# A new written-out order for a two-layer long-convolution and MLP kernel, with eight warm-up matmuls for six

## The chip, the cores and the metric

The kernel runs on one core of one Trainium2 chip. The metric is the device time of one execution in microseconds (us). Times are compared as medians of several runs; one further execution of each kernel is recorded by the hardware profiler, and every duration below comes from such a record. The engines are TensorE (PE; its weight loads are listed as PEld), VectorE (DVE), ScalarE (ACT), GpSimd (POOL) and SyncE (SP), which here issues nearly all transfers between memory (HBM) and the on-chip buffer. Matmul results land in PSUM, eight banks of 512 float32 columns on 128 partitions, and must be copied out by ACT or DVE.

## The reference

Inputs are bfloat16: a sequence of 2048 positions with 512 channels, filters, and a two-matrix MLP with 1376 hidden units. The result is four residual steps, a convolution mixer and an MLP, twice:

```python
def _A_ref(q, k, v, shift_k, ssm_k, ssm_D):
    for t in range(4):                                   # a short filter over k, by channel
        k_shift = k_shift + k_pad[:, t:t+S, :] * shift_k[:, 3-t][None, None, :]
    kv = k_shift * v
    y = irfft(rfft(pad(kv)) * rfft(pad(ssm_k)))[:S]      # a convolution 2048 long, by channel
    y = y + kv * ssm_D
    return q * y
def _B_ref(x, w1, b1, w2, b2):
    h = gelu(layernorm(x) @ w1 + b1)
    return h @ w2 + b2
x = A_q
for _ in range(2):
    x = x + _A_ref(layernorm(x), A_k, A_v, A_shift_k, A_ssm_k, A_ssm_D)
    x = x + _B_ref(layernorm(x), B_w1, B_b1, B_w2, B_b2)
```

The convolution's output doesn't depend on x, so it is computed once and used by both layers.

## The kernel before, in words

**The front** computes the convolution by matmuls with constant matrices. Each stage is made of tiles: one PE operation of several matmuls into one or two PSUM banks, and one copy of it by ACT or DVE (`evac`, line 453).

- *Filter* (tag `ht`): the filter arrives in four blocks (SP transfers 5 to 8, 512 KB each), is transposed on PE in four operations of 16 (62, 65, 68, 71, line 528), copied, and gets D added in one row (70, 73 and on POOL 64, 67).
- *First transform of the filter* (`h1`, line 545): 16 operations (74 to 104, even numbers) of 16 matmuls with 64 columns of weights, copied by the operation one number on.
- *Second transform* (`h2`, line 558): 16 operations (106 to 136) of 8 matmuls with the tables of transfers 28 to 43; then 16 transfers on chip (138 to 153) make a copy with the halves exchanged.
- *Short filter of k, times v* (`fir0` to `fir3`): channels 0 to 255 on PE (two transposes 154 and 168, line 589, with their copies 155 and 169; four filter operations 156, 158, 170, 172, line 606, each followed by a product with v on DVE, 157, 159, 171, 173, line 613); channels 256 to 511 on DVE (182 to 189 and 198 to 205, line 450, 16 passes of 2048 columns). They need the loads of k (10 to 19) and v (20 to 27).
- *First transform of kv* (`x1`, line 545), *second transform and product with the filter's* (`x2`, line 651, with a product on DVE each; the last is 268 or 274), *two inverse stages* (`i1`, line 674; `i2`, line 731).

**The two layers** run in blocks of 1 or 2 (first layer) and 4 (second layer) row tiles of 128 positions: statistics (line 754, 756) and norm (768) on DVE, a power on POOL (760, 762), the product with y and the addition to x on DVE (line 450), statistics and norm again, a transpose (tiles 0 and 1 on PE, line 814; all others by SP transfers, line 807), the first MLP matrix in 11 operations of 4 matmuls (`m1`, line 827) with a gelu each on ACT (line 832), the second one in three operations of 4, 4 and 3 matmuls per row tile (`m2`, line 860) and the addition to x on DVE (line 864). The last row tile's m2 is cut into 256, 128 and 128 columns (lines 849 and 853) with a transfer of the result after each.

**What sets the order.** Nothing is scheduled by the chip or by a library. Each operation gets a number in the order in which the program's text makes it. Then `arrange` goes through the tuple `ORDER`, 1114 numbers, and appends each operation to its engine's queue; each engine works its queue off strictly in order. An operation that two engines could do has a first and a second choice, and `SECOND` lists those that take the second. `BANKS` gives each PSUM tile its first bank; an operation that opens a tile waits for the copies out of the bank's former tile. `sync` derives the semaphore waits from the data dependences. So `ORDER`, `SECOND` and `BANKS` decide the sequence on every engine, SP's transfers included, and nothing else does.

**The warm-up**: POOL clears a row of zeros (operation 47, line 493) and one of ones (`one`, operation 49, line 504, a memset of 1 x 128); PE multiplies the zeros (operation 48, line 499) ahead of the filter's transposes, which are made to follow it.

Of the kernel before, what the change touches and what calls it, by code (L numbers as in the profile page):

```python
# [38 lines left out]
class Prog:  # L39
# [3 lines left out]

    G = 4
    ORDER = (
        0, 47, 8, 7, 48, 5, 3, 71, 68, 72, 73, 6, 1, 62, 98, 104, 16, 2, 69, 4, 65, 15, 63, 70, 64, 53, 102, 11, 13, 32, 49, 57, 99, 66,
        105, 100, 101, 80, 103, 50, 81, 17, 67, 76, 74, 56, 9, 51, 90, 52, 77, 94, 91, 96, 75, 19, 14, 12, 36, 95, 44, 18, 25, 27, 78, 60,
        61, 43, 10, 79, 35, 45, 26, 24, 88, 59, 86, 97, 82, 89, 42, 87, 92, 83, 41, 40, 33, 21, 84, 93, 182, 55, 168, 169, 85, 54, 154, 198,
        29, 155, 114, 30, 199, 120, 121, 31, 183, 58, 172, 136, 115, 173, 130, 116, 184, 137, 132, 28, 117, 158, 133, 108, 131, 200, 109,
        134, 106, 185, 22, 34, 135, 122, 23, 159, 123, 201, 186, 118, 20, 39, 156, 119, 107, 112, 202, 110, 157, 38, 37, 113, 111, 140, 126,  # L50
        46, 166, 203, 162, 187, 167, 170, 164, 127, 204, 124, 171, 163, 141, 165, 294, 128, 174, 139, 180, 129, 125, 176, 175, 181, 188,
        160, 178, 138, 177, 205, 189, 208, 161, 210, 209, 179, 145, 211, 196, 217, 212, 146, 220, 197, 310, 148, 218, 213, 190, 219, 221,
        144, 149, 143, 214, 215, 192, 142, 222, 147, 306, 194, 223, 193, 206, 224, 191, 195, 225, 229, 216, 235, 230, 231, 298, 207, 236,
        232, 233, 226, 296, 153, 260, 263, 304, 237, 227, 305, 257, 234, 275, 299, 228, 264, 261, 269, 254, 151, 258, 265, 244, 150, 255,
        333, 259, 276, 242, 240, 262, 300, 245, 243, 152, 256, 272, 266, 270, 248, 267, 277, 271, 273, 274, 307, 241, 246, 297, 268, 252,
        250, 247, 238, 251, 376, 253, 334, 377, 335, 292, 249, 302, 419, 477, 288, 336, 308, 378, 337, 421, 239, 420, 290, 422, 278, 379,
        293, 313, 289, 291, 314, 282, 286, 280, 529, 279, 479, 423, 380, 531, 284, 283, 424, 287, 281, 315, 381, 319, 285, 323, 430, 325,
        382, 425, 316, 338, 339, 295, 385, 317, 342, 324, 331, 340, 320, 383, 326, 301, 329, 341, 384, 303, 343, 478, 318, 344, 426, 386,
        332, 530, 431, 345, 330, 427, 346, 387, 347, 433, 480, 327, 348, 532, 349, 388, 432, 428, 389, 390, 533, 328, 429, 438, 435, 434,
        436, 321, 309, 481, 370, 534, 368, 391, 354, 439, 371, 369, 482, 437, 350, 440, 535, 356, 483, 366, 355, 441, 351, 442, 352, 358,  # L60
        357, 392, 360, 484, 364, 353, 367, 372, 445, 312, 393, 359, 443, 395, 399, 322, 409, 394, 397, 538, 583, 485, 486, 396, 407, 446,
        400, 365, 536, 633, 581, 362, 408, 398, 539, 489, 487, 488, 537, 635, 361, 490, 491, 444, 363, 403, 634, 401, 410, 405, 415, 404,
        413, 311, 636, 406, 373, 540, 492, 411, 582, 493, 451, 449, 461, 452, 450, 374, 453, 543, 541, 412, 402, 455, 494, 467, 584, 495,
        585, 462, 497, 459, 586, 542, 587, 414, 544, 468, 463, 465, 590, 447, 687, 454, 637, 460, 448, 545, 457, 588, 496, 591, 546, 416,
        549, 638, 592, 456, 473, 685, 417, 458, 498, 469, 642, 547, 464, 470, 466, 639, 686, 688, 519, 513, 589, 514, 595, 550, 375, 640,
        593, 474, 505, 548, 517, 511, 506, 737, 594, 499, 471, 518, 501, 738, 789, 418, 500, 596, 555, 512, 520, 643, 597, 641, 645, 502,
        646, 561, 475, 689, 598, 559, 472, 551, 644, 647, 560, 503, 690, 791, 569, 509, 557, 793, 599, 504, 691, 507, 552, 739, 515, 648,
        694, 510, 508, 476, 649, 570, 600, 571, 553, 692, 794, 516, 521, 522, 601, 693, 525, 790, 650, 651, 556, 565, 554, 740, 563, 602,
        567, 795, 741, 566, 572, 558, 697, 796, 526, 792, 742, 653, 573, 562, 797, 698, 609, 798, 652, 623, 615, 564, 527, 574, 568, 523,
        743, 616, 575, 528, 617, 607, 695, 618, 746, 696, 699, 605, 621, 744, 576, 577, 603, 700, 745, 608, 604, 622, 871, 578, 747, 701,  # L70
        613, 606, 611, 612, 624, 702, 748, 654, 749, 655, 619, 873, 524, 656, 669, 610, 799, 659, 620, 703, 579, 665, 629, 675, 751, 750,
        802, 869, 752, 614, 753, 754, 657, 704, 630, 666, 580, 663, 673, 660, 664, 667, 705, 631, 757, 875, 755, 674, 805, 706, 808, 658,
        661, 668, 800, 874, 632, 809, 801, 662, 870, 625, 872, 671, 670, 756, 876, 626, 877, 709, 758, 676, 806, 672, 707, 627, 681, 677,
        708, 803, 810, 759, 725, 771, 807, 628, 878, 678, 682, 760, 815, 761, 710, 683, 772, 816, 879, 719, 811, 949, 726, 880, 817, 679,
        720, 812, 804, 723, 951, 762, 763, 813, 724, 882, 684, 711, 950, 680, 715, 717, 955, 885, 775, 886, 881, 764, 712, 888, 814, 818,
        953, 727, 721, 954, 779, 887, 769, 895, 765, 780, 713, 819, 891, 889, 722, 766, 952, 896, 883, 714, 767, 716, 781, 728, 729, 820,
        890, 823, 827, 770, 824, 768, 897, 777, 718, 773, 956, 884, 892, 776, 774, 957, 778, 893, 825, 958, 962, 959, 828, 894, 826, 730,
        785, 733, 963, 898, 968, 782, 965, 821, 786, 787, 822, 899, 783, 969, 734, 843, 960, 900, 901, 841, 784, 731, 849, 907, 847, 735,
        961, 966, 732, 964, 903, 831, 833, 788, 1029, 905, 736, 1030, 837, 850, 967, 908, 848, 829, 844, 835, 904, 971, 906, 975, 1031,
        1033, 976, 902, 1035, 836, 839, 970, 977, 911, 909, 1034, 838, 973, 913, 972, 840, 1036, 919, 834, 1032, 842, 830, 1037, 925, 1038,  # L80
        926, 920, 912, 1045, 978, 923, 914, 845, 1048, 915, 927, 921, 1042, 832, 974, 979, 846, 910, 1039, 917, 1046, 980, 983, 855, 864,
        984, 1040, 922, 918, 928, 1041, 1043, 851, 924, 929, 1047, 1049, 985, 865, 856, 1050, 1044, 987, 916, 1057, 1051, 857, 1052, 866,
        860, 858, 981, 940, 982, 1053, 988, 1054, 1055, 986, 931, 1056, 930, 932, 1058, 861, 1059, 1060, 933, 935, 944, 934, 989, 995, 941,
        1061, 942, 1062, 867, 990, 1009, 1065, 945, 852, 853, 1003, 936, 1004, 937, 996, 1001, 1063, 1002, 943, 991, 862, 1005, 1064, 1067,
        854, 938, 997, 1066, 1010, 999, 993, 1068, 1069, 863, 1081, 939, 992, 946, 947, 1085, 1000, 1077, 1071, 948, 994, 1006, 1070, 1087,
        1079, 1088, 1083, 998, 1073, 1078, 1007, 1020, 1074, 1075, 1082, 1008, 1089, 1024, 1080, 1072, 1086, 1076, 1015, 1016, 1090, 1084,
        1108, 1100, 1111, 1017, 1021, 1112, 1011, 1109, 1095, 1025, 1096, 1018, 1026, 1012, 1097, 1101, 1013, 1113, 1022, 1027, 1102, 1014,
        859, 868, 1098, 1019, 1091, 1023, 1110, 1103, 1028, 1104, 1092, 1093, 1094, 1105, 1099, 1106, 1107)
    SECOND = (
        63, 64, 66, 67, 69, 70, 72, 77, 85, 89, 91, 97, 101, 161, 179, 191, 197, 213, 251, 283, 324, 392)  # L90
    BANKS = (
        0, 2, 0, 2, 2, 0, 4, 0, 4, 6, 0, 2, 2, 6, 6, 4, 2, 0, 4, 4, 0, 6, 4, 6, 0, 6, 2, 6, 0, 4, 6, 4, 4, 6, 4, 2, 2, 0, 0, 2, 0, 4, 6, 2,
        2, 6, 0, 6, 0, 6, 0, 2, 6, 2, 4, 6, 2, 2, 4, 2, 0, 0, 4, 0, 0, 0, 4, 6, 2, 0, 2, 4, 2, 6, 0, 4, 2, 4, 2, 6, 2, 6, 4, 0, 2, 4, 0, 2,
        6, 0, 6, 4, 4, 0, 0, 4, 4, 2, 6, 0, 6, 2, 2, 0, 6, 3, 1, 3, 0, 5, 1, 2, 6, 2, 6, 7, 7, 3, 7, 2, 1, 2, 3, 3, 4, 3, 4, 7, 2, 5, 2, 5,
        1, 0, 0, 0, 4, 3, 3, 0, 1, 4, 2, 5, 4, 5, 6, 5, 4, 2, 2, 3, 7, 2, 2, 5, 4, 0, 7, 3, 5, 1, 4, 7, 6, 0, 0, 5, 4, 1, 3, 2, 5, 1, 2, 1,
        2, 6, 6, 3, 4, 5, 6, 0, 1, 1, 6, 2, 0, 0, 4, 3, 4, 0, 2, 0, 2, 5, 3, 1, 1, 5, 5, 0, 5, 6, 0, 0, 1, 7, 1, 6, 1, 3, 4, 6, 2, 7, 3, 0,
        5, 2, 4, 6, 7, 1, 4, 2, 0, 7, 3, 4, 7, 5, 4, 3, 6, 7, 2, 7, 6, 1, 0, 3, 1, 2, 1, 4, 6, 2, 0, 3, 0, 1, 2, 5, 5, 5, 2, 2, 1, 0, 4, 7,
        4, 6, 1, 1, 2, 5, 7, 3, 0, 4, 2, 1, 3, 2, 2, 3, 1)


    def __init__(self, nc):
# [393 lines left out]
    tl = Tile(2)  # L495

    def f(e, tl=tl, z=z):
        for i in range(6):
            r = e.matmul(Q(tl, 0, 128, 0, [1, 512]), z[:, :128], z, start=True, stop=True)
        return r  # L500
    warm = P.op(PE, f, reads=[z], tile=tl)
# [399 lines left out]
```

## Time and profile before

| | before |
|---|---|
| median of 3 runs (lowest to highest) | 243.98 us (243.57 to 245.47) |
| the profiled execution's own time | 242.91 us |
| its span, first to last instruction | 241.1 us |
| PE busy (2330 matmuls) | 228.3 us, 95% |
| DVE busy | 172.7 us, 72% |
| ACT busy | 140.0 us, 58% |
| granted TensorE clock | 1.00 |

The span leaves out 1.8 us around the instructions. Rows of the timeline and of the chain of waits begin with the start and the length of a piece in us; "x16" counts the instructions merged into it; brackets give the idle time before it and what ended it ("issue": nothing that the profile shows). A row of the waits reads: engine and line that waited, what it waited for, us in total, times, the longest. PE busy is a modelled figure, since matmuls overlap: what counts is the distance between the starts. The trace also has each transfer's landing and the transfers that bring PE's instructions (queue q8: 18 packets, 0.29 MB).

### The profile page before, as it was taken

What the parts mean: (1) busy time and instruction counts of PE and PEld (TensorE: products, weight loads), DVE (VectorE), ACT (ScalarE), POOL (GpSimd) and SP (SyncE); (2) the same over time, 40 slices, a digit from 0 to 9 for tenths busy, and PEclk for the clock granted to TensorE, in tenths of its full rate; (3) what the DMA queues carried; (4) which work ended last, traced back from release to release, by engine and by line L of the source; (5) the groups of instructions that cost most, each with busy time, mean ns of one, the idle gap of its engine ahead of it and who ended that gap; (6) DMA issues with size and microseconds to landing.
All of it is one profiled execution on the core that took longest, in us unless ns stands there. A gap on an engine that the chain in (4) does not pass through costs nothing.

```text
span 241.1 us, 5575 instructions
## 1 busy us (share of the span) xinstructions
PE 228.3 (95%) x2330; PEld 152.5 (63%) x2330; DVE 172.7 (72%) x358; ACT 140.0 (58%) x225; POOL 37.6 (16%) x78
## 2 busy tenths in 40 slices
PE   6996999887899999999999999999999999999995
PEld 3985777675799887577667658644444444444543
DVE  0799699999999999999699789968772532100133
ACT  2397999999999995446426524703584013638000
POOL 1283000000004260603411201220120100000000
DMA  6999924999992001220301110223110332010204
GB/s 239 352 380 365 386 77 121 294 229 290 336 382 65 3 7 39 45 46 13 76 0 26 34 31 3 44 45 65 24 22 0 65 68 65 0 43 0 101 0 163
DMA packets 37035, 27.40 MB, mean 114 GB/s; under 512 B 19506, under 2 KB 29969, under 8 KB 37010
## 3 DMA queue, kind: packets, MB, share of 16 engines
q1 hardware_dynamic: 36446, 26.91, 37.3%
q8 instruction: 18, 0.29, 0.5%
q10 hardware_dynamic: 564, 0.14, 0.4%
q14 instruction: 7, 0.06, 0.1%
HBM read 16.82 MB, written 2.10 MB: 78 GB/s over the span
## 4 chain that ended last, share of the span: by engine, by line
PE 79%; DVE 8%; ACT 8%; DMA 2%; issue 2%; DVEq 0%
PE ps L827 32%; PE ps L860 31%; ACT ar L453 8%; DVE ar L450 5%; PE ps L674 5%; PE ps L731 3%; PE ps L528 2%; PE ps L545 2%; DVE ar L613 2%; DMA ar<-in_A_ssm_k_dram 2%; PE ps L651 2%; PE ps L849 1%; DVE ar L453 1%; PE ps L589 1%; PE ps L606 1%
## 5 line engine op out<-in xcount | busy, mean ns | idle before, releaser
L832 ACT ACTIVATE ar<-ps,sm 128x256 bf16<-128x256 f32 (+5 forms) x143 | 64.2, 523 | 71.3 <-PE ps L827 58.1
L827 PE MATMUL ps<-ar 128*128 128x256 bf16 (+5 forms) x572 | 82.6, 297 | 0.1
L860 PE MATMUL ps<-ar 128*128 128x512 bf16 (+1 forms) x341 | 79.9, 379 | 0.0
L453 ACT ACTIVATE ar<-ps 128x1024 bf16<-128x1024 f32 (+3 forms) x81 | 74.7, 1059 | 8.4 <-PE ps L545 6.5
L827 PEld LDWEIGHTS ps<-ar 128*128 128x128 bf16 (+1 forms) x572 | 53.0, 100 | 29.5 <-ACT ar L832 0.8
L450 DVE TENSOR_TENSOR ar<-ar 128x512 bf16<-128x512 bf16 (+3 forms) x105 | 63.5, 637 | 0.5 <-ACT ar L453 0.2
L860 PEld LDWEIGHTS ps<-ar 128*128 128x128 bf16 (+1 forms) x341 | 33.0, 98 | 34.5 <-ACT ar L832 0.2
L864 DVE TENSOR_TENSOR ar<-ar,ps 128x512 bf16<-128x512 bf16 x31 | 20.9, 683 | 34.9 <-PE ps L860 34.8
L754 DVE BATCH_NORM_STATS2 sm<-ar 128x6 f32<-128x512 bf16 (+1 forms) x68 | 42.5, 649 | 0.2
L768 DVE TENSOR_SCALAR ar<-ar,sm 128x512 bf16<-128x512 bf16 x64 | 24.9, 409 | 5.9 <-POOL sm L762 3.1
L760 POOL TENSOR_SCALAR sm<-sm 128x2 f32<-128x2 f32 (+2 forms) x26 | 6.0, 233 | 139.3 <-DVE sm L756 138.7
L762 POOL TENSOR_TENSOR sm<-sm 128x2 f32<-128x2 f32 (+2 forms) x26 | 20.6, 794 | 2.2
L545 PE MATMUL ps<-ar 128*64 128x128 bf16 x512 | 18.0, 221 | 1.8 <-ACT ar L453 1.2
L545 PEld LDWEIGHTS ps<-ar 128*64 128x64 bf16 x512 | 15.0, 110 | 4.5 <-ACT ar L453 2.5
L453 DVE CAST ar<-ps 128x1024 bf16<-128x1024 f32 (+1 forms) x14 | 16.3, 1180 | 0.5 <-PE ps L545 0.2
L674 PE MATMUL ps<-ar 128*128 128x128 bf16 x256 | 15.0, 220 | 0.6 <-ACT ar L453 0.6
L674 PEld LDWEIGHTS ps<-ar 128*128 128x128 bf16 x256 | 14.6, 114 | 0.8 <-ACT ar L453 0.8
L651 PE MATMUL ps<-ar 128*128 128x64 bf16 x256 | 9.9, 194 | 2.6 <-ACT ar L453 2.5
L853 DVE TENSOR_TENSOR ar<-ar,ps 128x128 bf16<-128x128 bf16 (+1 forms) x3 | 0.9, 330 | 14.0 <-PE ps L849 14.0
L651 PEld LDWEIGHTS ps<-ar 128*128 128x128 bf16 x256 | 8.2, 98 | 4.2 <-ACT ar L453 3.9
L453 DVE COPY ar<-ps 128x2048 bf16<-128x2048 bf16 (+1 forms) x5 | 5.2, 1062 | 7.8 <-PE ps L528 7.8
L756 DVE BATCH_NORM_AGGREGATE sm<-sm 128x2 f32<-128x6 f32 (+1 forms) x64 | 10.2, 172 | 0.4
(34 smaller groups left out, 85.2 us busy)
## 6 DMA issues: line engine op xcount, KB each, us to landing
ar<-tab_s SPq DMA_DIRECT2D x16, 256.0 KB, 9.9
ar<-ar SPq DMA_DIRECT2D x16, 256.0 KB, 5.2
ar<-in_A_ssm_k_dram SPq DMA_DIRECT2D x4, 512.0 KB, 5.3
ar<-in_A_k_dram SPq DMA_DIRECT2D x8, 256.0 KB, 7.2
ar<-in_A_v_dram SPq DMA_DIRECT2D x8, 256.0 KB, 9.9
ar<-in_A_q_dram SPq DMA_DIRECT2D x4, 512.0 KB, 6.1
out_dram<-ar SPq DMA_DIRECT2D x7, 256.0 KB, 2.0
ar<-in_B_w_dram SPq DMA_DIRECT2D x1, 1376.0 KB, 8.7
```

Of the source, the lines that this page charges most:

```text
L450: return P.op(eng, lambda e: e.tensor_tensor(o, a, b, op), reads=[a, b] + list(more), writes=[o])
L453: f = {ACT: lambda e: e.activation(dst, src(), AF.Copy), DVE: lambda e: e.tensor_copy(dst, src())}
L545: r = e.matmul(Q(tl, 64 * ri, 64, i * 128, [1, 128]), w, m, start=True, stop=True)
L651: r = e.matmul(Q(tl, 0, 128, i * pitch, [1, n]), w, m, start=True, stop=True)
L674: r = e.matmul(Q(tl, 0, 128, i * 128, [1, 128]), w, m, start=q == 0, stop=q == 1)
L754: P.op(DVE, lambda e, sj=sj, x=x: e.bn_stats(sj, x), reads=[x], writes=[sj])
L762: P.op(POOL, lambda e: e.tensor_tensor(r, v, hf, ALU.pow), reads=[v, hf], writes=[r])
L768: P.op(DVE, lambda e: e.tensor_scalar(o, x, m, r, ALU.subtract, ALU.mult), reads=[x, m, r], writes=[o])
L827: r = e.matmul(Q(tl, 0, rows, 0, [1, w]), a, m, start=dk == 0, stop=dk == 3)
L832: P.op(ACT, lambda e, dst=dst, tl=tl, rows=rows, bias=bias, w=w: e.activation(dst, Q(tl, 0, rows, 0, [1, w]), AF.Gelu_apprx_tanh, bias=bia ...
L860: r = e.matmul(Q(tl, 0, 128, 0, [1, 512]), ins[fc][0], ins[fc][1], start=fc == 0, stop=fc == 10)
L864: P.op(DVE, lambda e, x=x, tl=tl: e.tensor_tensor(x, x, Q(tl, 0, 128, 0, [1, 512]), ALU.add), reads=[x], writes=[x], tile=tl)
```

## The change

Three tuples are replaced and one number is changed; the program's arithmetic and tiles stay as they are.

```diff
     ORDER = (
-        0, 47, 8, 7, 48, 5, 3, 71, 68, 72, 73, 6, 1, 62, 98, 104, 16, 2, 69, 4, 65, 15, 63, 70, 64, 53, 102, 11, 13, 32, 49, 57, 99, 66,
...
+        49, 0, 47, 8, 7, 1, 3, 6, 48, 14, 71, 68, 5, 72, 18, 17, 15, 12, 4, 69, 9, 70, 50, 16, 65, 13, 19, 94, 2, 53, 73, 96, 51, 52, 11,
...
     SECOND = (
-        63, 64, 66, 67, 69, 70, 72, 77, 85, 89, 91, 97, 101, 161, 179, 191, 197, 213, 251, 283, 324, 392)
+        63, 64, 66, 67, 69, 72, 89, 97, 105, 127, 155, 161, 169, 175, 177, 215, 221, 239, 291, 349, 392)
     BANKS = (
-        0, 2, 0, 2, 2, 0, 4, 0, 4, 6, 0, 2, 2, 6, 6, 4, 2, 0, 4, 4, 0, 6, 4, 6, 0, 6, 2, 6, 0, 4, 6, 4, 4, 6, 4, 2, 2, 0, 0, 2, 0, 4, 6, 2,
...
+        0, 4, 2, 2, 0, 2, 2, 0, 6, 6, 0, 0, 4, 2, 4, 4, 0, 6, 4, 0, 2, 6, 2, 0, 6, 0, 4, 4, 2, 0, 2, 2, 4, 6, 0, 6, 4, 4, 4, 0, 6, 0, 2, 0,
...
     def f(e, tl=tl, z=z):
-        for i in range(6):
+        for i in range(8):
             r = e.matmul(Q(tl, 0, 128, 0, [1, 512]), z[:, :128], z, start=True, stop=True)
```

What the new tuples do to the queues, by operation number:

- *PE's front, before:* 48, 71, 68, 62, 98, 104, 65, 102, 100, 80, 50, then nine h1 tiles (76 to 84), 168, 154, then h2 tiles with the filter operations 172, 158, 156, 170 among them.
- *PE's front, after:* 48, 71, 68, 50, 65, 94, 96, 92, 62, 100, 104, 90, 88, 84, 78, 86, 76, 102, 168, 98, 82, 74, 80, 154, 172, 120, 110, 116, 112, 124, 158, 106, and so on. The changes between 64-column and 128-column matmuls on PE fall from 20 to 14.
- *Copies moved from DVE to ACT:* h1 77, 85, 91, 101; x1 179, 191, 197, 213; i1 251, 283; i2 324. *From ACT to DVE:* h1 105; h2 127; the shift copies 155 and 169; x1 175, 177; x2 215, 221; i1 239, 291; 349 (the transpose of row tile 0). The add 70 goes from POOL to DVE.
- *SP, before:* filter blocks 8, 7, 5, 6, then k, tables and v mixed. *After:* 8, 7, 6, one k, 5, the seven other large k, 11, a bias, a table, 10, then v and tables. Among the later loads the second MLP matrix (303) now precedes the first (302).
- *ACT:* its table load (operation 4) comes before the small load 2 instead of after it; the taps' copies 51 and 52 come before all h1 copies.
- *POOL:* 49 comes before 47.
- *PE in the layers:* the m1 and m2 operations are interleaved differently; the first m1 of the third and later blocks stands earlier or later by up to some ten operations. *The end:* PE's last operations are 1105 (256 columns) and then 1108 (128 columns); before, 1105 was last.

## The prediction

> **What bounds the kernel now.** I read the chain of waits first, then the table of who waited for whom, then the timeline of the first 30 us. From 66 us on the chain is TensorE (PE) alone, without a gap over 0.3 us, up to 238.5 us:
>
> ```profile
> 66.05 8.35 PE ps L674 x144
> 74.40 0.44 PE ps L731 x4
> ...
> 224.96 12.33 PE ps L860 x57
> 237.29 1.22 PE ps L849 x11
> 238.51 0.02 issue
> 238.53 0.42 DVE ar L853
> ```
>
> PE's matmuls are the same after the change (two warm-ups apart), so the time can only change by the time PE stands idle, and nearly all of that lies before 66 us, where the chain runs through ScalarE (ACT) and VectorE (DVE) emptying PSUM. Four rows of the timeline show the start:
>
> ```profile
> 1.31 2.74 PE L499 MATMUL ps<-ar 128*128 128x512 bf16 x6 [1.31 <-POOL ar L493]
> 4.84 4.56 PE L528 MATMUL ps<-ar 128*128 128x128 bf16 x48 [0.80 <-DMA ar<-in_A_ssm_k_dram]
> ...
> 10.02 1.94 ACT L453 ACTIVATE ar<-ps 128x1024 bf16<-128x1024 f32 x2 [6.23 <-PE ps L545]
> ...
> 23.02 0.94 PE L589 MATMUL ps<-ar 128*128 128x128 bf16 x14 [2.28 <-issue]
> ```
>
> The last one is a stop in which PE waited for nothing but its own instructions. The trace's queue q8 carries 18 instruction blocks of 16,384 bytes; in the quiet later part one starts per about 259 PE instructions. Counted back, the second block was asked for near instruction 407 (about 15.0 us), started only at 20.54 us behind the tables' loads, took 1.11 us, and PE went on at 23.02 us, instruction 705. The waits show who paid for it:
>
> ```profile
> DVE ar L613 <- PE ps L606: 2.1, 1, 2.1
> ...
> ACT ar L453 <- PE ps L589: 1.5, 1, 1.5
> ```
>
> DVE's idle time up to its last filter product (268, ending 70.23 us) is 10.4 us: 6.81 before its first copy, 0.16 + 0.80 + 0.21 after it, 2.05 at the stop, 0.4 in crumbs. ACT starts at 10.02 us and loses 1.46 at the stop.
>
> **The start.** POOL now clears `one` before the warm-up's zeros: one small memset, 0.19 us and 0.27 from start to start in the trace. Warm-ups begin at 1.31 + 0.27 = 1.58 us; started 0.427 us apart, eight end at 4.96. The first filter block lands at 4.80 and its transposes began at 4.84, so they begin 0.12 us later. But PE no longer stands still before them. Now its matmuls stop streaming at 3.85 and idle 1.0 us; the transposes then start 107 ns apart, and at 8.25 us, 3.41 us after the restart, the spacing falls to 60 ns. If steady work from 1.58 earns the full clock after the same 3.41 us, the first 32 transposes (PE 71 and 68) run at 60 ns: PE 71 takes 1.16 us to its end instead of 1.93. DVE then starts at 6.17, not 6.81. The gain for the h1 stage's first ACT copy is worth about 0.5 us (9.54 against 10.02), since PE 68 still waits for its block (landed 6.08). Bounds: 1.5 us (32 x 47 ns) and -0.12. I take the 0.64 of DVE.
>
> The Trainium skill, "TensorE: Matmul & The Clock Gate", Part 1, says that the window of 3.4 us runs freely and is not started by the kernel, so the place where the clock rises varies between executions. No run here shows that; the row's 3.41 us from the restart fits a restart as well. By the rule the DVE gain would lie anywhere from -0.1 to 0.64, and the sum below would be 0.3 smaller on average.
>
> **The front to the stop.** Copies cost, from start to start in stretches without waits: ACT 0.90 us, DVE 1.13 for an h1, h2 or x tile, 1.14 for a DVE product or a copy of 16 transposed blocks, ACT 1.88 for that same copy; PE takes 0.45 for an h1 or h2 tile, 0.9 for a shift transpose, 1.74 for a shift filter.
> - *DVE.* Copies 72 and 69 and the two adds behind them end at 8.95; 66, 97, 63, 105, 89 follow to 15.0, with 0.3 of waiting for PE 62. Then 198 needs all k. The k loads now stand ahead of all v and table loads; the eighth is SP's 12th load, with 4 MB up to and including it; the transfer that closed 4 MB before landed at 16.07. So DVE waits 1.1 us more, then runs 198, 182 and the shift copy 169 to 19.5. Both shift copies (169, 155) come over from ACT; four h1 copies (77, 85, 91, 101) go to ACT, one (105) comes back.
> - *ACT.* The two taps copies (1.07 us) move ahead of the h1 copies, into its idle start. Thirteen h1 copies from 9.54 with about 1.0 of waiting for banks that DVE or ACT itself must empty end at 22.3.
> - *PE.* The block asked for near instruction 407 is asked for where PE starts 78 (it waits for DVE's 105), about 13.9 instead of 15.0. With the same 5.5 us in the queue, 1.1 of transfer and 1.4 until PE goes on, it is there at about 21.7. PE reaches that point, the start of shift 154, at 20.3 (80 waits for DVE's 169) and stops 1.4 instead of 2.28 us.
> - *After the stop.* PE's 154 (0.9) and 172 (1.74) end at 24.2, the first h2 tile at 24.7: ACT's first h2 copy is at 24.8, before 25.77; ACT has idled 2.5 us there, but with 0.9 us less ahead of it in all. DVE has 183, 199, 184 and 155 to do meanwhile, idles 0.25, and starts 173 at 24.25, before 26.63. Its idle time to that point is 6.17 + 0.05 + 0.3 + 1.1 + 0.25 = 7.9 us against 10.1, with one more shift product done.
>
> **From there to the MLP.** DVE's list up to its last product (now 274) is as long as before: 59.0 us against 58.8 summed from the rows. The moves of h2, x1, x2 and i1 copies cancel (seven to DVE, six to ACT; ACT is 0.9 lighter). Its 43.2 us from 24.25 end at 67.5. Crumbs of 0.3 allowed, I take 2.4 us earlier than 70.23. The swaps (16 SP transfers, about 0.7 apart) start when the ninth ACT h2 copy ends, near 33 us instead of 37.87, and everything SP issues behind them, W1 and W2 too, follows no later; W2 landed at 74.98 and is first used at 87.5. The first gelu matmul waits for the norm of tile 0 on DVE: 12.7 us of DVE work after the product against 12.8; its copy, now DVE's, ends at +15.2 instead of PE's +14.8. So the MLP starts 2.0 us earlier.
>
> **In the MLP** PE takes some blocks sooner, and DVE (the third pair of numbers in these rows by stage: busy us of the ten, and instructions) has little to spare:
>
> ```profile
> 90.00:100.00 10.00, 10.00 (x85) 7.26 (x83) 9.43 (x29) 6.98 (x21) 2.27 (x6) 1.00 0.20 40
> 100.00:110.00 10.00, 9.86 (x70) 6.61 (x69) 9.90 (x27) 3.42 (x8) 3.07 (x6) 1.00 0.23 45
> ```
>
> So I compare sums ahead of each block's last norm (DVE) and first matmul (PE), with DVE's real pace 6% over the rows:
> - block 2: DVE +2.6, PE +1.5. Norm 89.5 + 2.8 - 2.4 = 89.9, transfer 2.5: 92.4, against 92.8 + 1.5 = 94.3: room for a gain of 1.9.
> - block 3: DVE -1.4, PE -3.1. Norm 94.6, with transfer 97.2, against 99.6: room for 2.4.
> - block 4: DVE +6.4, PE +4.2. Norm 103.1 + 6.8 - 2.4 = 107.5, with transfer 110.1, against 111.5: room for **1.4**.
> - block 5: room for 3.2; later ones for more, and in layer two the shortest way (PE 942 to block 22) has 4.3 us of PE work over 1.1 of DVE and 2.5 of transfer.
>
> So PE stops briefly for blocks 2 and 4 and 1.4 us are left. Changes between 64- and 128-column tiles fall from 20 to 14; one costs about 0.1 us (155 ns between starts instead of 55), but they lie before 66 us, where PE waits for ACT and DVE anyway: nothing, at most 0.6. At the tail the last matmul group is the 128-column one (PE 1108): DVE's last add is 0.29 instead of 0.42 us, so -0.1. Two more warm-ups (0.85 us) lie in the wait for the filter; without that cover they cost what step one says.
>
> **Sum:** -1.4 - 0.1 = -1.5 us on the profiled execution (span 241.1, its own time 242.91): 241.4. That execution lies 1.07 below the median of the runs shown, 243.98; on the median the forecast is **242.5**.
>
> **Rivals.** *All of the front comes through* (-3.0, 241.0): DVE's real order overtakes my sums in the MLP, blocks 2 and 4 don't wait, and the block of instructions arrives before PE needs it (2.4 + 0.6). For it: ACT is lighter and DVE has five shift products to hide the stop. Against: DVE's 9.9 of 10 us busy at 100 to 110 us. *Nothing arrives earlier* (-0.3, 243.7): the clock rises as late as before and the instruction block is not there before 23 us, since its request falls into the same crowded queue; then ACT's first h2 copy comes at 26.2, later than now, and only DVE's extra product is left. *PE starves in the MLP* (+2.9, 246.9, the slower side): PE's order reaches blocks 2, 3 and 4 with 6.7, 6.4 and 6.4 us less PE work than DVE work ahead of them, where it was 5.6, 4.7 and 4.2. Each microsecond that DVE waits between 67 and 107 us, for POOL's powers (3.1 us in three waits now, up to 1.4 each) or for an ACT copy, goes straight into the time. It decides once such waits pass 1.4 us in all; three more of 1.4 give 4.2 - 1.4 = +2.8, plus the late start of 0.1. *The change does not do what it says*: the stop at the 705th instruction stays 2.3 us long; that is the second rival.
>
> **How the numbers follow.** Forecast 0.50, all of it 0.22, nothing 0.13, starved 0.15. About 1% (2.44 us, below 241.5 or above 246.4) is what a measurement of this kernel can tell from no change. Faster 0.22 + 0.03 of the forecast's lower edge = 0.25; slower 0.15; the same 0.60. The range 240.4 to 246.0 leaves out the far half of the starved case and the edge of the fast one.
>
> **What would show it.** Right: transposes 60 ns apart from about 5 us; DVE's first copy near 6.2; an issue stop of PE under 1.5 us near 20 to 22 us; the last product near 67.5 us; the first gelu matmul near 83; waits of PE under 1 us each for transposed blocks 2 and 4. Wrong: PE waits of several us between 85 and 115 us, DVE waiting for POOL or k loads, or a second issue stop.

## The result, and the profile after

The changed kernel takes **241.39 us** (median of 11 runs, 240.63 to 242.62) against 243.98 for the kernel before on the same chip (median of 11, 243.02 to 245.47): a ratio of 0.990, 95% interval 0.987 to 0.993, so 1.0% less. Ratios and their intervals leave out executions that lie over 1.5% above the fastest of their kernel; medians take in all. The forecast was 242.5, in a range from 240.4 to 246.0. The profiled execution took 240.63 us with a span of 238.8, against 242.91 and 241.1: **2.3 us less**, where 1.5 was forecast on that scale.

The chain of waits of the changed kernel (start and length in us, what ran), from the filter products on:

```profile
41.46 0.60 SPq L439
...
47.53 4.19 DMA ar<-ar
...
59.08 5.80 ACT ar L453 x6
64.88 0.05 issue
64.92 6.56 PE ps L674 x112
71.49 0.44 PE ps L731 x4
...
234.55 1.84 PE ps L849 x22
236.39 0.02 issue
236.41 0.29 DVE ar L853
```

As before, PE alone carries the chain from about 65 us, and it gets there earlier (the first inverse row at 64.92, 66.05 before). New on the chain is the row of SP transfers that exchange halves (L439) between 41 and 48 us; an experiment comes back to it. The last piece is 0.29 instead of 0.42 us.

The start, in the timeline (start, length, engine, line; in brackets the idle time before and what ended it):

```profile
1.56 3.33 PE L499 MATMUL ps<-ar 128*128 128x512 bf16 x8 [1.56 <-POOL ar L493]
...
4.78 2.52 PE L528 MATMUL ps<-ar 128*128 128x128 bf16 x32
6.04 2.54 DVE L453 COPY ar<-ps 128x2048 bf16<-128x2048 bf16 x2 [6.04 <-PE ps L528]
...
9.61 1.94 ACT L453 ACTIVATE ar<-ps 128x1024 bf16<-128x1024 f32 x2 [0.66 <-PE ps L545]
...
15.60 1.47 PE L545 MATMUL ps<-ar 128*64 128x128 bf16 x45 [0.79 <-issue]
...
16.42 2.36 DVE L450 TENSOR_TENSOR ar<-ar 128x2048 bf16<-128x2048 bf16 x2 [1.28 <-DMA ar<-in_A_k_dram]
...
22.08 1.01 PE L589 MATMUL ps<-ar 128*128 128x128 bf16 x15 [1.31 <-issue]
```

The transposes follow the warm-up without a gap and DVE starts at 6.04 (6.81 before). Then DVE waits 1.28 us for the loads of k. PE stops for its own instructions twice, before 15.60 and before 22.08. Counted from start to start the second stop takes 1.54 us (2.50 before). Both lie behind the same counted PE instructions as in the kernel before, the 449th and the 705th; the first took 0.25 us there and takes 1.01 now.

DVE's waits up to its last filter product tell where the front's time went. All are idle times of single DVE operations in the trace, in us:

| DVE waits for | before | after |
|---|---|---|
| first copy (72) | 6.81 | 6.04 |
| later copies of the filter and of h1 (69, 66 or 63, 77) | 1.17 | 0.26 |
| loads of k (198) | 0 | 1.28 |
| filter product 172 behind the stop (173) | 2.05 | 0.33 |
| an h2 tile (127) | 0 | 0.34 |
| all waits above 0.08 | 10.3 | 8.33 |
| last product ends | 70.23 | 68.21 |

DVE's work between the waits is the same, 59.9 us, with the add 70 now part of it (before, 64, 67 and 70 are all on POOL). So the 2.0 us that the front gains are 2.0 us of waiting, and most of them come from the stop, which now has DVE's shift products and copies beside it. Of the 1.7 us that DVE gains by its earlier start (0.77) and by shorter waits in its next copies (0.91), the k loads take back 1.28.

The MLP by stretches of ten us: behind the length of the stretch the busy us (and instructions) of PE, of PE's weight loads, DVE, ACT and POOL, then the granted clock and the transfers:

```profile
90.00:100.00 10.00, 9.95 (x78) 7.50 (x78) 9.58 (x28) 5.30 (x16) 3.22 (x6) 1.00 0.25 48
100.00:110.00 10.00, 9.95 (x63) 6.00 (x63) 9.96 (x29) 4.68 (x13) 3.83 (x8) 1.00 0.15 30
```

PE stays full although DVE is at 9.96 of 10 us. The first gelu matmul starts at 83.08 (85.04), the last PE operation ends at 236.37 (238.50).

### The profile page after: what moved, and what is told of

The parts are those of the page before. It is cut to its first block, busy times and chain, and to the rows that moved or that the text cites. A ratio compares the mean times of both kernels' runs of the same rounds, so it can differ in the third digit from the quotient of the medians.

```text
span 238.8 us, 5555 instructions
## 1 busy us (share of the span) xinstructions
PE 226.2 (95%) x2312; PEld 151.6 (63%) x2332; DVE 171.6 (72%) x359; ACT 138.3 (58%) x225; POOL 41.3 (17%) x77
## 3 DMA queue, kind: packets, MB, share of 16 engines
q1 hardware_dynamic: 36446, 26.91, 37.8%
## 4 chain that ended last, share of the span: by engine, by line
PE 77%; ACT 9%; DMA 4%; DVE 4%; SPq 3%; issue 3%; ACTq 0%
PE ps L860 31%; PE ps L827 30%; ACT ar L453 9%; PE ps L674 5%; PE ps L731 3%; SPq L439 3%; PE ps L545 3%; DMA ar<-in_A_ssm_k_dram 2%; DVE ar L453 2%; DMA ar<-ar 2%; PE ps L528 1%; PE ps L606 1%; PE ps L849 1%; DVE sm L754 1%; PE ps L589 1%
## 5 line engine op out<-in xcount | busy, mean ns | idle before, releaser
L832 ACT ACTIVATE ar<-ps,sm 128x256 bf16<-128x256 f32 (+4 forms) x143 | 64.7, 525 | 72.5 <-PE ps L827 68.1
L827 PE MATMUL ps<-ar 128*128 128x256 bf16 (+4 forms) x568 | 84.2, 297 | 0.2
L860 PE MATMUL ps<-ar 128*128 128x512 bf16 (+1 forms) x329 | 79.0, 379 | 0.6
L453 ACT ACTIVATE ar<-ps 128x1024 bf16<-128x1024 f32 (+1 forms) x81 | 72.5, 1057 | 9.0 <-PE ps L511 4.5
L762 POOL TENSOR_TENSOR sm<-sm 128x2 f32<-128x2 f32 (+2 forms) x26 | 21.6, 832 | 2.2
L545 PE MATMUL ps<-ar 128*64 128x128 bf16 x512 | 17.1, 221 | 1.4 <-issue 0.8
L674 PE MATMUL ps<-ar 128*128 128x128 bf16 x256 | 15.0, 220 | 0.6 <-ACT ar L453 0.6
L453 DVE CAST ar<-ps 128x1024 bf16<-128x1024 f32 x11 | 13.0, 1212 | 0.3 <-PE ps L558 0.3
L453 DVE COPY ar<-ps 128x2048 bf16<-128x2048 bf16 (+1 forms) x8 | 8.2, 1024 | 6.4 <-PE ps L528 6.3
L558 PE MATMUL ps<-ar 128*128 128x128 bf16 x128 | 8.6, 220 | 0.8 <-ACT ar L453 0.8
```

The source lines that it names most:

```text
L453: f = {ACT: lambda e: e.activation(dst, src(), AF.Copy), DVE: lambda e: e.tensor_copy(dst, src())}
L545: r = e.matmul(Q(tl, 64 * ri, 64, i * 128, [1, 128]), w, m, start=True, stop=True)
L674: r = e.matmul(Q(tl, 0, 128, i * 128, [1, 128]), w, m, start=q == 0, stop=q == 1)
L762: P.op(POOL, lambda e: e.tensor_tensor(r, v, hf, ALU.pow), reads=[v, hf], writes=[r])
L827: r = e.matmul(Q(tl, 0, rows, 0, [1, w]), a, m, start=dk == 0, stop=dk == 3)
L832: P.op(ACT, lambda e, dst=dst, tl=tl, rows=rows, bias=bias, w=w: e.activation(dst, Q(tl, 0, rows, 0, [1, w]), AF.Gelu_apprx_tanh, bias=bia ...
```

## The experiments

Times are medians. Each is compared with runs of the kernel before on the same chip, which took 243.87 us in the first group of four (32 runs), 243.44 in the second (23) and 243.59 in the third (21). The hybrids' first two, `new_six` and `old_eight` are the first group; the kernels with six loads queued and the hybrids with banks exchanged the second; `new_pool`, the two with eight loads queued and `new_one` the third. A mean granted clock of 0.993 in an execution stands for one window of 3.41 us at half clock (0.5 x 3.41 of 243 us is 0.7%; the profiles of `old_eight` and `new_cap6` show one each). The kernel before shows one in 17 of these 76 runs; they took 245.15 to 246.21 us, the others 242.21 to 244.83. Where such runs make up much of a median, that is said. PE's waits at the seam of the hybrids and in the MLP are counted from start to start, less one matmul's usual distance; the bracket in a row is up to 0.2 us smaller, since it counts from the modelled end of the matmul before.

**Front and MLP apart.** The order, engines and banks of one kernel up to the first gelu matmul, those of the other behind it.

```diff
     ORDER = (
...
-        343, 384, 426, 344, 385, 345, 386, 530, 346, 387, 347, 319, 388, 318, 432, 389, 330, 428, 348, 483, 349, 320, 390, 327, 354, 427,
...
+        343, 384, 426, 344, 385, 345, 386, 530, 346, 387, 347, 319, 388, 318, 432, 389, 330, 428, 348, 483, 349, 320, 390, 327, 427, 433,
...
```

`front_new_mlp_old`:

> The changed kernel's order, engines and banks up to its first gelu matmul (with eight warm-ups), the old order, engines and banks for all the rest. Theory "the front carries the gain, the MLP order only passes it on": the first gelu matmul starts near 83.1 us as in the changed kernel (85.05 before), and the old MLP order keeps all of the 2.0 us, about -2.0 us against the kernel before. Rival "the MLP order carries part of it": half or less comes through, -1.2 us or nearer to zero.

Measured: 243.42 us (12 runs), ratio 0.9975 (0.9947 to 1.0004); the first gelu matmul stands at 84.99.

`front_old_mlp_new`, the other way round (the seam lies 391 operations into the old order):

> The other half: the old order, engines, banks and six warm-ups up to near the first gelu matmul, the new order, engines and banks behind it. Theory "the front carries the gain": first gelu matmul near 85 us as before, time -0.2 us against the kernel before (the shorter tail, 2.62 instead of 2.84 us from the last matmul group on), between -0.4 and +0.3. Rival "the MLP order carries part": -1.0 us or more. If the new order starves PE for lack of a head start, it is slower by 0.5 or more.

Measured: 245.64 us (9 runs), ratio 1.0062 (1.0021 to 1.0103).

Neither tells the theories apart. At the seam PE waited 1.73 and 1.81 us for a bank that ACT had still to empty, a cost of the seam. So in two further kernels all tiles that open behind the seam have the PSUM banks 2 and 4, and 3 and 5, exchanged.

`front_new_mlp_old2`:

> As the first hybrid (new front, old MLP order), but with the PSUM banks 2, 3 and 4, 5 exchanged for all tiles behind the seam, so that the first matmul behind it no longer waits 1.73 us for ScalarE's copy out of its bank. Theory "the front carries the gain": -2.0 to -2.4 us against the kernel before in executions of equal clock (the first hybrid's -0.6 plus the 1.73). Rival "the old MLP order has no room": DVE's blocks come late and it stays at -1.3 us or nearer to zero.

Measured: 242.02 us (6 runs), ratio 0.9941 (0.9917 to 0.9964), -1.4 us. In its profile the MLP's first matmul is 1.49 us earlier than before (83.56; in this execution the front itself was 0.5 us later than in the one of the changed kernel), PE waits another 0.61 us for a bank at the seam, and ends 1.02 us earlier (237.48). After that no wait of PE is over 0.3 us, so the old MLP order passes on what the front gives. By the times alone this is less clear: -1.4 lies between the theory's -2.0 and the rival's -1.3, and the late front of that one execution doesn't account for the median.

`front_old_mlp_new2`:

> As the second hybrid (old front, new MLP order), with the same banks exchanged behind the seam, so that the wait of 1.81 us there goes. Theory "the front carries the gain": within 0.4 us of the kernel before. Rival "the new MLP order asks for more DVE head start than the old front gives": PE waits for transposed block 2 or for VectorE's copies by 0.5 us or more, and it is slower than the kernel before by that.

Measured: 246.59 us (6 runs), ratio 1.0102 (1.0059 to 1.0145): the rival, slower. PE waits 1.25 us for DVE's copy 392 near the seam and 0.98 us at 134 us for DVE's addition 576. So behind the old front the new MLP order is no gain. That it needs DVE's earlier arrival is not shown: the first wait lies at the seam, and the second comes back below in a kernel whose front is 0.7 us earlier than that of the changed kernel.

**The warm-ups.** One number:

```diff
-        for i in range(8):
+        for i in range(6):
```

`new_six`, the changed kernel with six:

> The changed kernel with six warm-ups, nothing else. Both the restart theory (the clock rises 3.41 us after PE starts again) and the profile agree that the 32 first transposes go back to 107 ns and DVE's first copy to about 6.7 to 6.8 us (6.04 with eight). If the clock's window ran freely, the first transposes would in some executions still be at 60 ns. Price: theory "covered": DVE waits for the k loads until 16.4 anyway (1.3 us with eight) and ACT runs out of h1 copies before PE's stop, so only the stop can move: +0.0 to +0.4 us against the changed kernel. Rival "uncovered": the 0.6 us at DVE's start comes through, +0.6 us. The stop behind PE's 705th instruction should stay at that instruction, now two transposes or matmuls further on in the program, if it hangs on the instruction count, and stay at the same operation if it is a wait of that operation.

`old_eight`, the kernel before with eight:

> The kernel before with eight warm-ups, nothing else. The transposes should run 60 ns apart from 4.97 us if unbroken warm-up is what gives the clock, DVE's first copy near 6.2 instead of 6.81. Theory "the stop follows the request": everything up to the stop is 0.5 us earlier, so PE's instruction block is asked for earlier, with fewer loads ahead of it, and PE goes on near 22.4 instead of 23.02: -0.4 to -0.7 us against the kernel before. Rival "the block is served at a fixed place in the loads' queue": PE goes on at 23.0 and the time is within 0.2 us of before.

`new_one`, the changed kernel with one:

> The changed kernel with one warm-up instead of eight. From the executions so far: with eight the clock rises 4.2 to 6.5 us after the start, with six 5.0 to 9.3. Theory "a free window of 3.41 us must be mostly busy": with one it can rise only after a window full of transposes, at 8 to 12 us; the first transposes run at 107 ns and VectorE's first copy starts at about 6.8 us or later. VectorE's wait for the k loads (1.28 us) takes up most of that: +0.2 to +0.8 us against the changed kernel. Rival "the warm-ups don't matter": within 0.2 us. Rival "the warm-ups carry the gain": +1.5 us or more.

| warm-ups, kernel | median (runs) | ratio to before | clock rises at | first 16 transposes |
|---|---|---|---|---|
| 8, changed | 241.39 (11) | 0.990 | 4.49 us | 4.78 to 6.00 |
| 6, changed | 242.86 (12) | 0.9938 (0.9901 to 0.9975) | 5.02 | 4.90 to 6.13 |
| 1, changed | 245.35 (12) | 1.0031 (0.9994 to 1.0067) | 14.55 | 5.06 to 6.98 |
| 6, before | 243.98 (11) | 1 | about 8.2 | 4.84 to 6.77 |
| 8, before | 244.47 (12) | 1.0011 (0.9982 to 1.0039) | 6.37 | 4.86 to 6.65 |

The column on the clock comes from the trace's records of the granted clock (where a trace has none, as that of the kernel before, from the spacing of the transposes, 107 or 60 ns). It refutes what I had expected of the mechanism. With six warm-ups and 0.8 us of idle PE behind them the clock rose 0.12 us after PE's restart; with eight unbroken ones it rose 5.06 us after the first. Over all profiles, eight give a rise between 4.23 and 7.02 us (eight executions), six between 5.02 and 9.2 (five). The Trainium skill, "TensorE: Matmul & The Clock Gate", Part 1, says that the window of 3.4 us runs freely and isn't started by the kernel. This agrees: in `old_eight` the changes of the clock lie at 6.37, 23.43 and 26.85 us, five windows of 3.41 us apart and then one.

So more warm-ups buy a likelier early clock, not a sure one. The price of losing it is seen with one warm-up: 4.0 us more than with eight by the medians, 3.2 by the ratios (half of its runs have a half-clock window too). In its profile (an execution of 247.79 us, 2.4 above the median) the clock stays low until 14.55, although PE counts as busy throughout the window before the last, 7.72 to 11.14; what a window needs to raise the clock is left open by these runs. DVE's product 198 comes at 18.94 instead of 16.42, and PE waits 1.60 us for a transposed block and 1.03 us for the addition 576 in the MLP.

The step from eight to six costs 1.5 us by the medians, 0.9 by the ratios, but its profile gives the clock no part in that. DVE starts 0.13 us later. What else differs are 0.6 us by which the k loads landed later in that execution, and a wait at 131 us that comes up below. The stop stayed behind instruction 705, as expected.

`old_eight` gained nothing. Its profile shows why, in windows cut at its own clock's edges (busy us of PE, weight loads, DVE, ACT and POOL; then the granted clock):

```profile
16.61:20.02 3.41, 3.34 (x97) 2.94 (x92) 3.41 (x4) 3.35 (x5) 3.13 (x4) 1.00 1.07 335
20.02:23.43 3.41, 1.08 (x21) 0.96 (x19) 3.41 (x4) 2.32 (x2) 0.31 (x2) 1.00 1.05 372
23.43:26.85 3.42, 3.42 (x28) 2.81 (x26) 0.94 (x1) 2.79 (x3) 0.00 (x0) 0.50 1.07 391
```

The stop of 2.55 us (20.21 to 22.76) fell whole into one window, in which PE was busy for 1.08 us. In the next one the clock is 0.50, and the product 172 takes 2.56 us instead of 1.9. Ten of its 12 runs have a mean clock of 0.993 (0.992 in two of them), against 17 of 76 with six warm-ups; why so many more, these runs don't show. The block of instructions itself came 0.3 us earlier (20.24 instead of 20.54): about the rival's fixed place in the queue.

**The stop.** Each front load on SP waits for the landing of the load six (or eight) places before it:

```diff
             assert all(self.ops[p].eng is not None for p in o.preds)
+        loads = [o for o in self.order[SP] if o.i < 47]
+        for o, p in zip(loads[6:], loads):
+            o.preds[p.i] = "raw"
```

`old_cap6`, the kernel before:

> The kernel before with the same limit of six loads in the queues. Theory "instructions behind loads": the stop of 2.28 us at 23 us goes, and with it the 3.41 us at half clock that follow it in about a third of the executions (those with a mean granted clock of 0.993, 245.2 to 246.2 us); profiled time about -1.5 to -2.3 us, median -1.8 to -2.8 us. Then most of what the changed front gained is to be had without any new order. Rival "PE's own stop": no change.

Measured: 241.93 us (12 runs), ratio 0.9960 (0.9933 to 0.9988). The block's transfer starts at 17.95 instead of 20.54, and PE passes instruction 705 without a stop; DVE's 173 starts at 24.64 instead of 26.63. PE's row of the shift transposes, which broke at 23.02 before, is now in one piece:

```profile
19.58 1.96 PE L592 MATMUL ps<-ar 128*128 128x128 bf16 x32
```

The nine runs at full clock have a median of 241.83, against 243.43 for those of the kernel before: -1.6 us without any new order. Over all runs it is -1.5, less than the -1.8 to -2.8 expected. Three runs still have a half-clock window; what makes it there, no profile shows.

`new_cap6`, the changed kernel:

> The changed kernel, with one addition: each of the front's loads on SyncE waits until the load six places before it has landed, so that no more than six stand in the queues. Theory "PE's block of instructions waits behind the queued loads": q8's second transfer starts about 2 us after its request instead of 5.6 us, so it is there by about 18.5 us, before PE needs it at 20.5; the stops behind PE's instructions 449 (1.01 us) and 705 (1.54 us) go to 0.3 us or less, PE is never idle for most of a 3.41 us window, and no execution shows the mean granted clock of 0.993. The loads land when they did before (last k load near 16.4 us). Time: -0.5 to -1.3 us against the changed kernel, -3.1 to -3.9 us against the kernel before. Rival "the stop is PE's own (a fixed cost of crossing into a new block)": the stops stay at 1.0 and 1.5 us and the time is that of the changed kernel. Rival "the k loads bound this part": stops vanish, but DVE's wait for the k loads (until 16.4 us) sets what follows, and the time falls by 0.3 us or less.

Measured: 244.31 us (12 runs), ratio 1.0016 (0.9985 to 1.0046): 2.9 us slower than the changed kernel (six runs with a half-clock window). The stop at instruction 705 did go (the block's transfer starts at 17.54), the one at 449 fell only from 1.01 to 0.62 us, and another wait took the place of the first. Three rows of its timeline:

```profile
19.34 5.15 POOL L523 TENSOR_SCALAR ar<-ar,sm 128x128 bf16<-128x128 bf16 x4
20.46 1.07 PE L592 MATMUL ps<-ar 128*128 128x128 bf16 x16
24.32 3.00 PE L609 MATMUL ps<-ar 128*128 128x384 bf16 x13 [2.80 <-POOL ar L523]
```

(Lines are 3 higher in this kernel.) PE's shift transposes end unhindered at 21.5, and then the filter product 172 waits 2.80 us for the diagonal 58, the last that it needs of POOL. This idle window too is followed by half clock (23.59 to 27.0), so that 172 takes 3.0 us. In the changed kernel 58 ends at 22.57, 0.57 us ahead of 172's first recorded matmul at 23.15: it was next in line behind the stop. The same diagonals there:

```profile
14.56 1.99 POOL L520 TENSOR_SCALAR ar<-ar,sm 128x128 bf16<-128x128 bf16 x3
16.62 0.10 POOL L710 MEMSET sm<- 128x4 f32 x1
16.81 7.07 POOL L520 TENSOR_SCALAR ar<-ar,sm 128x128 bf16<-128x128 bf16 x4
```

Three take 0.6 us each; of the next four, two take 2.36 and 2.61 (and the last, beside one product, 1.22). Both of the long ones end 0.39 us after a pair of DVE products with two on-chip operands (198 and 182, 183 and 199; ends at 18.78 and 22.19), and it is so in `new_cap6` (18.70 and 22.10; POOL at 19.09 and 22.49). The Trainium skill, "SBUF — State Buffer", section "SBUF: two separate sides", says that GpSimd and such a DVE operation share one pair of ports, and that the one which holds it locks the other out for its whole instruction. The rows agree, and show the GpSimd operation kept out through two DVE products in a row.

**POOL ahead, fewer loads queued, two copies moved.**

```diff
     ORDER = (
...
-        49, 0, 47, 8, 7, 1, 3, 6, 48, 14, 71, 68, 5, 72, 18, 17, 15, 12, 4, 69, 9, 70, 50, 16, 65, 13, 19, 94, 2, 53, 73, 96, 51, 52, 11,
-        92, 66, 305, 62, 95, 100, 97, 67, 104, 93, 63, 28, 64, 90, 88, 105, 10, 101, 26, 44, 45, 84, 91, 24, 56, 78, 85, 79, 86, 33, 59, 76,
-        89, 57, 87, 198, 77, 36, 102, 168, 60, 103, 35, 25, 98, 30, 27, 31, 82, 74, 310, 182, 54, 169, 80, 61, 29, 183, 58, 199, 99, 37, 22,
+        49, 0, 47, 8, 7, 1, 3, 6, 48, 14, 71, 68, 5, 72, 18, 17, 15, 12, 4, 69, 9, 70, 50, 16, 65, 13, 19, 94, 2, 53, 58, 73, 96, 51, 52,
+        11, 92, 66, 305, 62, 95, 100, 97, 67, 59, 60, 61, 104, 93, 63, 28, 64, 90, 88, 105, 10, 101, 26, 44, 45, 84, 91, 24, 56, 78, 85, 79,
+        86, 33, 76, 89, 57, 87, 198, 77, 36, 102, 168, 103, 35, 25, 98, 30, 27, 31, 82, 74, 310, 182, 54, 169, 80, 29, 183, 199, 99, 37, 22,
...
```

Operations 58 to 61 leave their later places; the rest keeps its order.

`new_pool`:

> The changed kernel with four of GpSimd's eight filter diagonals (58 to 61) moved ahead into its idle time at 9 to 13 us; nothing else. In the profile after, two diagonals that fall beside VectorE's shift products take 2.35 and 2.62 us instead of 0.61, and the filter product 172 on TensorE has its last diagonal at 22.58. Theory "GpSimd waits for VectorE's products": all eight take about 0.61 us and are done by about 17 us. As the instruction stop ends at 22.09 and TensorE's 154 ahead of 172 at 23.10, the diagonals are not what 172 waits for: time 0.0 to -0.3 us against the changed kernel. Rival "the diagonals bound the restart": -0.5 us or more.

Measured: 241.52 us (6 runs), ratio 0.9907 (0.9871 to 0.9943): no change against the changed kernel. All eight diagonals take 0.60 to 0.61 us, the last ends at 17.00, and the stop stays, 1.46 us. As long as the stop is there, the diagonals cost nothing.

`new_cap8_pool`, the same and the limit of above with 8 in place of 6:

> The changed kernel with the diagonals moved ahead and at most eight loads in the queues (each front load waits for the landing of the one eight places before). Theory: with six the stop went, but TensorE then waited 2.80 us for the diagonal 58, which fell beside more of VectorE's products; with the diagonals done early it waits for neither, 154 ends at about 21.6 and 172 at about 23.5 us (24.84). VectorE is busy with products until 24.55 all the same, so only its 0.33 us of waiting go, and ScalarE's 1.5 us do not reach the end: -0.2 to -0.6 us against the changed kernel, and no half-clock window. Rival "fewer loads in the queues starve the tables": h2 matmuls wait for tables, no gain or slower.

Measured: 241.35 us (8 runs), ratio 0.9899 (0.9861 to 0.9938); no run has a half-clock window. The mechanism is as expected: 154 ends at 22.02 and 172 at 23.77 (23.09 and 24.84 in the changed kernel), the last product at 67.48 (68.21), the first gelu matmul at 82.34 (83.08). Still the time is that of the changed kernel, where 0.2 to 0.6 us less were expected: 0.77 us are lost at 129 us, in the same wait as with six warm-ups. No kernel has a limit of six and the diagonals early, so that the diagonals make up the loss of `new_cap6` is read from its 2.80 us of waiting and was not tested apart from the limit.

`new_cap8_pool_moved`, two copies more that change engines:

```diff
     SECOND = (
-        63, 64, 66, 67, 69, 72, 89, 97, 105, 127, 155, 161, 169, 175, 177, 215, 221, 239, 291, 349, 392)
+        63, 64, 66, 67, 69, 72, 87, 89, 97, 105, 127, 161, 169, 175, 177, 215, 221, 239, 291, 349, 392)
```

> As the one before, and two copies change engines: the h1 copy 87 goes to VectorE, into its 1.28 us of waiting for the k loads, and the shift copy 155 goes to ScalarE, into its 2.58 us of waiting behind the h1 copies. Theory "what bounds is VectorE's list of work up to its last product": it becomes 1.1 us shorter where it counts, 173 starts near 23.5 instead of 24.88, the last product ends near 66.9 instead of 68.21: -1.2 to -1.8 us against the changed kernel, below both kernels. Rival "PSUM or the transfers bound behind 25 us": the start of 173 moves, but the last product does not.

Measured: 241.80 us (8 runs), ratio 0.9928 (0.9897 to 0.9960): the rival. 173 starts at 24.04, 0.84 us earlier than in the changed kernel, and the last product ends at 68.20. From 173 to the last product DVE now waits 0.98 us, against 0.35 in the changed kernel: 0.34 for the h2 tile in both, and for two more tiles of PE, 0.31 us at 48.20 and this one:

```profile
28.93 1.22 DVE L616 TENSOR_TENSOR ar<-ps,ar 128x1024 bf16<-128x1024 f32 x1 [0.26 <-PE ps L609]
```

The rest of the 0.84 us is in still smaller distances. (Lines are 3 higher here too.) So from here on, by these rows, PE's tiles come hardly ahead of DVE, and no sum of mine contained that. The transfers that exchange halves stand on the chain of the changed kernel (L439), but DVE's products don't wait for them there: of the four that product 237 needs, the last landed at 52.62, and 237 started at 53.91 in a row of DVE operations without a gap. In all nine profiles with the new front the last product ends 19.2 to 19.7 us after SP issues transfer 143, but in the five with the old front it is 23.4 to 23.8, so this even distance doesn't show which of the two sets the other. No kernel was run that moves PE's tiles or those transfers alone.

**The wait at 125 to 131 us.** Two profiles, the changed kernel with eight and with six warm-ups, in the same row of the timeline (a norm on DVE that waits for an SP transfer which transposes):

```profile
126.72 0.41 DVE L768 TENSOR_SCALAR ar<-ar,sm 128x512 bf16<-128x512 bf16 x1 [2.50 <-DMA ar<-ar]
```

```profile
129.08 0.41 DVE L768 TENSOR_SCALAR ar<-ar,sm 128x512 bf16<-128x512 bf16 x1 [4.21 <-DMA ar<-ar]
...
131.06 1.90 PE L860 MATMUL ps<-ar 128*128 128x512 bf16 x8 [0.97 <-DVE ar L864]
```

From issue to landing this transfer (706) took 2.45 us in the first and 4.16 in the second, and there PE then waits for DVE's 576, which is queued behind the norm. The difference is where one of PE's instruction blocks falls: its transfer started 0.21 us before the issue of 706 in the first and 1.18 us after it in the second. The 14 profiles hold 420 such transposing transfers:

| instruction block's transfer starts | transfers | from issue to landing |
|---|---|---|
| not between 1.5 us before and 2.5 us after the issue | 356 | median 2.47 us, 2.39 to 3.52 |
| 1.5 to 0.45 us before | 5 | 2.43 to 2.52 |
| 0.45 before to 0.3 after | 15 | median 2.72, 2.42 to 3.40 |
| 0.3 to 2.1 us after | 31 | median 3.82, 3.18 to 4.31 |
| 2.1 to 2.5 us after | 13 | median 2.49, once 4.28 |

In all seven profiles in which 706 took 3.8 us or more, PE waited 0.8 to 1.3 us for 576 (three with six warm-ups and the new MLP order, and those of `new_one`, `new_cap6`, `new_cap8_pool` and `new_cap8_pool_moved`). In the two others with the new MLP order, of the changed kernel and `new_pool`, it did not wait there. Which transposes meet a block depends on how many instructions PE has had and when. That the meeting decides was read from these profiles; no kernel was run that moves only the block.

## Why the prediction was right, and where it was not

**Start: right in its numbers, wrong in its cause.** Warm-ups from 1.56 (1.58 was said), DVE from 6.04 (6.17), ACT's first h1 copy at 9.61 (9.54). The step "if steady work from 1.58 earns the full clock after the same 3.41 us" fell: the restart that I took from one row isn't what the clock counts from, and the skill's rule, which I had set aside, is the one that the later profiles bear out. That the number fits was luck: in the eight profiles with eight warm-ups DVE's first copy starts anywhere from 6.04 to 7.06.

**The wait for k: right.** 198 at 16.42 (16.1), a wait of 1.28 us (1.1).

**The stop: right in place and length, incomplete in number.** The 705th instruction in operation 154, reached at 20.54 (20.3), 1.54 us (1.4). Not foreseen was the stop behind instruction 449, 1.01 us: the block ahead of it is asked for among the same queued loads, and I had counted only the second. A second issue stop was one of my own signs of being wrong. The cause, blocks that wait behind the queued loads, was shown by both kernels with six loads queued. My sentence on what comes after the stop left out POOL's diagonals; only because the stop stayed did that cost nothing.

**The last product: mis-sized by 0.4.** 68.21 instead of 67.5 (67.8 with the crumbs), a gain of 2.0 instead of 2.4. DVE's 173 was 0.63 us later than said, though its idle time to that point, 8.0 us, was as forecast (7.9): the work ahead of it is 0.5 us longer than my sum of rows. The wait of 0.34 us for an h2 tile is about the 0.3 of crumbs.

**MLP start: right, by two misses that cancel.** 83.08, a gain of 1.97 us (2.0). I had the last product 0.4 us too early and took 0.4 off again for tile 0's copy on DVE (15.2 us after the product instead of 14.8); it took 14.87, against 14.82 before.

**The room in the MLP: the step that failed.** "Room for 1.4" at block 4 should have cut the 2.0 us. Block 4 was indeed the tightest place: its last half landed at 109.19 and PE started on it at 109.24. But nothing was cut, so the room was 2.0. The term that was mis-sized is "+6.8", DVE's added work ahead of that norm, 6.4 by the rows with 6% on top. From the last product to the norm's end DVE took 32.84 us before (70.23 to 103.07) and takes 38.44 now (68.21 to 106.65): +5.6. That is 0.8 less than my sum of rows even without the 6%. Successive DVE instructions overlap: in that stretch their durations add up to 37.8 us in 32.84 before and to 44.4 in 38.44 now, +6.6, near my sum. DVE's idle time there hardly differs (0.90 and 1.15 us), so it doesn't explain the miss. Where the 6% came from stays open.

**Tail and tile changes.** From the end of PE's last matmul to the end of the span 2.45 instead of 2.62 us, -0.17 (said: -0.1). Fewer changes of tile width show in no wait of PE behind 66 us.

**The sum.** -1.97 for the front, all of it passed on, -0.16 between the first gelu matmul and PE's end, -0.17 for the tail: -2.3 in all, against -1.5 said. The rival "all of the front comes through" was half right: the MLP passes all, but the block of instructions did not arrive in time. Its 241.0 lies nearer to the measured 241.39 than my 242.5. "PE starves in the MLP" didn't happen, and is closer than I gave it credit for: with the same MLP order and the front 0.6 us later, PE waits a microsecond at operation 625, which none of my sums had looked at; `new_cap8_pool` waits there with an earlier front too. The 2.6 us between the medians are 0.3 more than between the two profiled executions. Of the runs behind them four of the kernel before took 245.29 to 245.47 us, the length of its half-clock executions elsewhere, and two of the changed kernel have such a window (242.39 and 242.62); without these six the medians are 243.57 and 241.27, 2.3 us apart like the profiles.

## What to carry to other kernels

Look for "issue" in the waits of PE while loads are queued, count back to when its instruction block was asked for, and try a limit on the loads in flight before a new order: here three lines gained 1.5 us where the new order and the warm-ups gained 2.6. When a stall is to go, list everything that its consumer needs and when each is there: behind PE's stop came POOL's diagonals, and behind those DVE's waits for other tiles of PE. And add up work from start to start, not by durations: DVE's overlap, and here that made 5.6 us look like 6.6.

## What was not expected of the hardware

- PE's clock fell to half for 3.41 us after a window in which PE was busy for 1.08 of 3.41 us (`old_eight`), and after one in which it was busy for 1.36 (`new_cap6`), at the edges of a grid of 3.41 us (6.37, 23.43 and 26.85 in the first). The same page of the Trainium skill gives an idle window as the condition; here PE was not idle for all of it. A stop can thus cost more than its length, in some executions and not in others.
- The transfer of one 16 KB block of PE's instructions lengthens a transposing transfer on chip from 2.47 us to between 3.2 and 4.3 when it starts 0.3 to 2.1 us after that one's issue.
- A GpSimd operation of 0.61 us took up to 2.61 us beside two DVE products and ended 0.39 us after them.
